# The last output tile in two halves added to a copied sum, and a newly fitted order of issue, in a fused attention and two-layer kernel

## The chip, the cores and the metric

The kernel runs on one NeuronCore of a Trainium2 chip. Times are microseconds (us) on the device. What counts is the median time of an execution. TensorE is called PE, its weight loads PEld, VectorE DVE, ScalarE ACT, GpSimd POOL and SyncE SP.

## The reference

Three steps follow each other. For batch 2, 8 heads, 768 positions and head size 64, block attention: each query sees the keys less than 16 positions away, and 24 summaries of blocks of 32 (the maximum of the keys, the mean of the values).

```
k_sum = k.reshape(B, H, nb, block, D).max(axis=3)
v_sum = v.reshape(B, H, nb, block, D).mean(axis=3)
mask_l = np.abs(pos[:, None] - pos[None, :]) < window
scores_all = np.concatenate([scores_l_m, scores_s], axis=-1)
a = np.exp(scores_all); a = a / (np.sum(a, axis=-1, keepdims=True) + 1e-09)
return np.matmul(a, v_all)
```

The result, as 1536 tokens of 512 features, goes through a gated layer of width 1536 and then through a second layer of width 2048:

```
xn = x / rms * rms_g
x = (silu(xn @ w_gate) * (xn @ w_val)) @ w_out
h = x @ w_in
out = where(h > 0, h, exp(min(h, 0)) - 1) @ w_out2
```

The weights are given in 64-bit floating point; activations and the output are in 32-bit.

## The kernel before

The 1536 tokens are three blocks of 512. `add_pair` does the attention of 128 queries (a pair of 64-query tiles, as two tiles of four heads): loads and transposes q, forms scores (`scores`, for the first four pairs on top of a mask laid in PSUM by `premask`), takes row maxima and exponentials, normalises (`normalize`), transposes (`turn_e`) and multiplies by v (`apply_v2`), and copies into the block's `xT`. The v windows are four buffers `va0` to `va3`, whose lower rows hold the block means; `place_v` puts the means into the first and `repeat_v` copies them on.

`add_norm` scales a block by the root of its mean squares. In the first block it works on two halves of 256 tokens: `square` (ACT) squares two groups of features at a time into two tiles, `sum_square` (PE) sums them over the features by products with ones, `root` (POOL) takes the power, `diagonal` (DVE) and `spread` (PE) lay it out over the features, and `scale_x` (DVE) multiplies. `SUMS = 2` says that for the halves PE sums both square tiles; with 1, `add_square` (POOL) adds the second tile to the first before.

`add_block1` and `add_block2` are the two layers. Every operand of a product is split into a rounded part and a rest (`split_a`, `split_b`, `x_hi`, `x_lo`, `act_a`, `act_b`), and each product is three (`THREE`): high by high, high by low, low by high. The first layer runs over 12 chunks of its width, the second over 16: a projection of 12 products of 512 columns, the nonlinear step, and `down`, 12 products that add onto the four accumulators `a0` to `a3` (one PSUM bank each). Weights arrive as 64-bit words and become 32-bit ones in three or four steps (`convert_a` on ACT, `convert_b` to `convert_d` on DVE). For the first two chunks of the first block the projections run by halves of 256 tokens, so that they can begin when the first half is scaled.

At the end of the third block the last two chunks (14 and 15) are put into the accumulators one accumulator after the other. `copy_out` copies each accumulator to an `ob` tile and `store` writes it. For the last one, `copy_out` is cut in two halves of 256 columns, one for ACT and one for DVE, with a store for each, both issued by SP.

The order of all work comes from a planner, `Order`, that runs on the host while the kernel is built. `add` hands it an operation with an engine (or a choice of engines with a duration each), a due time, what it reads and writes and the buffers that it takes. `issue` simulates the engines, takes on each free engine the ready operation that is due first, and writes the instructions in that order; on the chip each engine runs its own list in that order, and semaphores hold it back where data is missing. A load has a duration on the one modelled queue. The due times are moved by a table, `SHIFT`, with one entry for a kind of operation in one of ten stretches of due time (`EDGES`), and by constants such as `TOFF`, `T0`, `QL`, `WARM_AT`; `FLEX` says from which tile on `normalize` may be on ACT, too.

## Time and profile before

| | us |
|---|---|
| median of the runs shown (645.16, 645.78, 648.27) | 645.78 |
| profiled execution | 646.54 |
| span of the profiled execution | 644.8 |
| PE busy in the span | 630.3 (98%) |
| DVE, ACT, POOL busy | 454.8, 342.4, 95.6 |

The span goes from the first instruction to the last one; 1.74 us of the execution lie around it. A busy time is the sum of the instructions' own times; a PE that is busy is not always at its peak. In a row of a timeline, what stands in square brackets is the idle time before it and what ended it. The granted clock of TensorE in the table of stages is a share of 2.4 GHz.

### The profile page before, as it was taken

The page shows a single profiled execution, that of the slowest core. Times are in us where ns is not written, and L with a number is a line of the kernel's source. Part 1 is how long each engine was busy: PE and PEld are TensorE (multiplying, and loading weights), DVE is VectorE, ACT ScalarE, POOL GpSimd, SP SyncE. Part 2 cuts the span into 40 slices and gives each one's busy share as a digit, 9 for nine tenths or more (in the row PEclk, how much of TensorE's full clock was granted, in tenths as well). Part 3 has the DMA queues.
Part 4 walks back from the last instruction along what each step waited for, and adds up shares of the span by engine and source line. Part 5 has one row for each costly group of instructions (what it writes and reads, how often), then busy time and mean ns, then how long its engine had stood idle before and what let it go on. Part 6 is the DMA issues. An engine that isn't in the chain of part 4 may idle for free.

```text
span 644.8 us, 9843 instructions
## 1 busy us (share of the span) xinstructions
PE 630.3 (98%) x3644; PEld 516.3 (80%) x3644; DVE 454.8 (71%) x828; ACT 342.4 (53%) x739; POOL 95.6 (15%) x160
## 2 busy tenths in 40 slices
PE   7899999999999999999999999999999999999997
PEld 5678777788888888888888888888888888888885
DVE  4788878868964557499999975555765555855554
ACT  2797568975463633465555564434444444544442
POOL 5753356363210210000000000000000000000000
PEclk9999999999999999999999999999999999999999
DMA  9998858565500000025656300000010000100001
GB/s 217 243 225 211 213 156 237 179 137 176 162 1 0 2 1 0 2 67 180 185 166 207 110 1 1 1 1 1 1 65 1 1 1 1 65 1 1 2 0 66
DMA packets 80352, 52.94 MB, mean 82 GB/s; under 512 B 51504, under 2 KB 75312, under 8 KB 80304
## 3 DMA queue, kind: packets, MB, share of 16 engines
q1 hardware_dynamic: 80304, 52.31, 29.9%
q8 instruction: 29, 0.48, 0.3%
q14 instruction: 19, 0.16, 0.1%
HBM read 49.15 MB, written 3.15 MB: 81 GB/s over the span
## 4 chain that ended last, share of the span: by engine, by line
PE 84%; DVE 6%; DMA 3%; SPq 3%; ACT 2%; issue 1%; DVEq 0%; ACTq 0%
PE acc L967 34%; PE ph L899 20%; PE pg L899 13%; PE pv L728 1%; PE pv_7c L899 1%; PE pv_8c L899 1%; PE pv_9c L899 1%; PE pv_11c L899 1%; PE pv_10c L899 1%; PE s L676 1%; PE pv_4c L899 1%; DMA va<-in_v 1%; DMA st_o<-in_moe_w_out 1%; PE pv_6c L899 1%; PE pv_1c L899 1%
## 5 line engine op out<-in xcount | busy, mean ns | idle before, releaser
L899 PE MATMUL ph<-xb,ws_i 128*128 128x512 f32 x576 | 137.9, 389 | 0.0
L967 PE MATMUL acc<-ws_p,act 128*128 128x512 f32 x576 | 137.7, 389 | 0.0
L967 PEld LDWEIGHTS acc<-ws_p,act 128*128 128x128 f32 x576 | 108.1, 188 | 22.5
L899 PEld LDWEIGHTS ph<-xb,ws_i 128*128 128x128 f32 x576 | 108.1, 188 | 22.4
L899 PE MATMUL pg<-x,ws_g 128*128 128x512 f32 (+1 forms) x456 | 108.7, 383 | 1.6 <-DVE ws_g L313 0.9
L967 PE MATMUL acc<-act,ws_o 128*128 128x512 f32 x432 | 106.3, 392 | 0.0
L899 PEld LDWEIGHTS pg<-x,ws_g 128*128 128x128 f32 x456 | 81.5, 188 | 19.1 <-DVE ws_g L313 1.3
L967 PEld LDWEIGHTS acc<-act,ws_o 128*128 128x128 f32 x432 | 80.4, 188 | 17.1 <-issue 0.5
L939 ACT ACTIVATE ex<-ph 128x512 f32<-128x512 f32 x48 | 28.8, 599 | 105.0 <-PE ph L899 105.0
L943 DVE TENSOR_SCALAR ex<-ex 128x512 f32<-128x512 f32 x48 | 20.5, 427 | 87.5 <-ACT ex L939 87.5
L302 ACT CAST act<-ex 128x512 fp32r<-128x512 f32 x48 | 29.8, 620 | 21.6 <-DVE ex L947 21.6
L302 ACT CAST ws_v<-raw_v 128x512 fp32r<-128x512 f32 x36 | 22.3, 620 | 32.6 <-PE acc L967 9.7
L932 DVE SCALAR_TENSOR_TENSOR th<-th,pg 128x512 f32<-128x512 f32 x36 | 24.6, 684 | 20.5 <-ACT th L928 20.3
L313 DVE TENSOR_TENSOR ws_i<-raw_i,ws_i 128x512 fp32r<-128x512 f32 x48 | 33.1, 689 | 8.0 <-ACT ws_i L302 8.0
L302 ACT CAST ws_i<-raw_i 128x512 fp32r<-128x512 f32 x48 | 29.7, 620 | 12.1 <-PE acc L967 12.1
L928 ACT ACTIVATE th<-pg 128x512 f32<-128x512 f32 x36 | 21.4, 595 | 26.7 <-PE pg L899 26.6
L313 DVE TENSOR_TENSOR act<-ex,act 128x512 fp32r<-128x512 f32 x48 | 33.1, 689 | 3.2 <-ACT act L302 0.7
L947 DVE SCALAR_TENSOR_TENSOR ex<-ph,ex 128x512 f32<-128x512 f32 x48 | 33.2, 691 | 1.5
L313 DVE TENSOR_TENSOR ws_p<-raw_p,ws_p 128x512 fp32r<-128x512 f32 x48 | 32.8, 682 | 1.2 <-ACT ws_p L302 1.2
L302 ACT CAST ws_p<-raw_p 128x512 fp32r<-128x512 f32 x48 | 29.6, 616 | 6.7 <-PE acc L967 6.7
L313 DVE TENSOR_TENSOR ws_o<-raw_o,ws_o 128x512 fp32r<-128x512 f32 x36 | 27.7, 770 | 6.3 <-ACT ws_o L302 6.2
L302 ACT CAST ws_o<-raw_o 128x512 fp32r<-128x512 f32 x36 | 22.3, 620 | 16.1 <-PE acc L967 3.5
(214 smaller groups left out, 918.8 us busy)
## 6 DMA issues: line engine op xcount, KB each, us to landing
st_i<-in_moe_w_in SPq DMA_DIRECT2D x16, 512.0 KB, 3.9
st_p<-in_moe_w_out SPq DMA_DIRECT2D x16, 512.0 KB, 3.8
st_g<-in_moe_w_gate SPq DMA_DIRECT2D x12, 512.0 KB, 4.9
st_o<-in_moe_w_out SPq DMA_DIRECT2D x12, 512.0 KB, 5.5
st_v<-in_moe_w_val SPq DMA_DIRECT2D x12, 512.0 KB, 4.9
va<-in_v SPq DMA_DIRECT2D x20, 192.0 KB, 5.6
kr<-in_k SPq DMA_DIRECT2D x12, 256.0 KB, 5.0
out<-ob SPq DMA_DIRECT2D x11, 256.0 KB, 2.0
```

The lines of the kernel that those rows point to most:

```text
L302: nc.scalar.copy(out=out, in_=in_)
L313: (nc.gpsimd if eng == POOL else nc.vector).tensor_sub(out, a, b)
L676: nc.tensor.matmul(pq[h][ts, pr, :], qb[hs, pr, ts], ka[n][hs, pr, :], start=not pre, stop=not pre or pr == NP - 1)
L728: nc.tensor.matmul(pv[64 * h:64 * h + 64, pr, n, :], va[:NK, 2 * pr + h, :], T[f"ats{b}_{j}_{h}"][:, pr, QT * n:QT * n + QT], start=True, ...
L899: nc.tensor.matmul(pt[:, i], wt[:, a, kk * P:(kk + 1) * P], xt[:, c, kk, i], start=(kk == 0 and n == 0), stop=(kk == KM - 1 and n == 2))
L928: nc.scalar.activation(out=new("t2", f"th{b}_{c}", [P, TB]), in_=T[f"pg{b}_{c}"], func=AF.Tanh, scale=0.5)
L932: nc.vector.scalar_tensor_tensor(th, th, 1.0, T[f"pg{b}_{c}"], op0=ALU.add, op1=ALU.mult)
L939: nc.scalar.activation(out=new("t2", f"ex{b}_{c}", [P, TB]), in_=T[f"ph{b}_{c}"], func=AF.Exp)
L943: nc.vector.tensor_scalar(ex, ex, 1.0, -1.0, op0=ALU.min, op1=ALU.add)
L947: nc.vector.scalar_tensor_tensor(ex, T[f"ph{b}_{c}"], 0.0, ex, op0=ALU.max, op1=ALU.add)
L967: nc.tensor.matmul(acc, lhsT, rhs, start=(first and n == 0), stop=(last and n == 2))
```

## The change

For the last tile (rows 384 to 511 of the third block), the products of chunk 15 go into two banks of their own, 256 columns each (`down_part`). The accumulator, then complete for the other fifteen chunks, is copied to `ob` in one piece, and `add_part` adds each half to the copy. The first half is stored by SP and the second by ACT.

The planner's duration of a load is raised: weights 1.52 to 1.56 and 1.64 to 1.72, q and (for the second batch) k 1.18 to 1.25, a window of v 0.95 to 1.05; that of `convert_d` 0.6 to 0.63. All the constants and the table of shifts are new. `SUMS` is 1, `FLEX` 8 instead of 10 (so that `normalize` for one more pair is for POOL alone), and `LO_0` has the rests of w_val in the first block on POOL alone, where the twelve of the profile were before as well.

```diff
-        add("SP", 1.52 if kind in "op" else 1.64, need - (14 if need > T0 + 20 else LEAD), fetch, kind, c, w=[st], new=[("st", st)])
+        add("SP", 1.56 if kind in "op" else 1.72, need - (14 if need > T0 + 20 else LEAD), fetch, kind, c, w=[st], new=[("st", st)])
...
-        add("SP", 0.95, due, load_v, b, t, w=[va + "#a"])
+        add("SP", 1.05, due, load_v, b, t, w=[va + "#a"])
...
+    def down_part(x, act, ws):
+        ot, wt = T[act], T[ws]
+        pt, cs = new(MM, f"end{x}", [P, TB // 2]), slice(x * TB // 2, (x + 1) * TB // 2)
+        for n, (a, e) in enumerate(THREE):
+            nc.tensor.matmul(pt, ot[:, a, 3 * P:], wt[:, e, cs], start=n == 0, stop=n == 2)
+
+    def add_part(x, ob):
+        out = T[ob][:, x * TB // 2:(x + 1) * TB // 2]
+        nc.vector.tensor_add(out, T[f"end{x}"], out)
...
-    def store(src, r0, cs):
-        nc.sync.dma_start(out=out[r0:r0 + P, cs], in_=T[src][:, cs])
+    def store(src, r0, cs, by):
+        (nc.scalar if by == ACT else nc.sync).dma_start(out=out[r0:r0 + P, cs], in_=T[src][:, cs])
...
+            add_down(names, act, ws, False, c == C2 - 1, False, due, [(m,) for m in range(3)])
+            if c == C2 - 2:
+                add_down(names, act, ws, False, True, False, due + 4.08, [(3,)])
+            else:
+                for x in range(2):
+                    add(PE, 0.36, due + 6 + 0.3 * x, down_part, x, act, ws, r=[act + "#h", act + "#l", ws + "#h", ws + "#l"],
+                        w=[f"end{x}"], new=[(MM, f"end{x}")])
...
-                where = ANY if parts == 1 else ({ACT: 0.27}, {DVE: 0.33})[x]
-                add(where, 0, end + 0.3 * m, copy_out, names[m], ob, cs, r=[names[m], ob], w=[f"{ob}#{x}"])
-                add("SP", 0.73, end + 2, store, ob, b * TB + m * P, cs, r=[f"{ob}#{x}"])
+            add(ANY, 0, end + 0.3 * m, copy_out, names[m], ob, slice(0, DM), r=[names[m], ob], w=[f"{ob}#{x}" for x in range(parts)])
...
+            for x in range(2):
+                add(DVE, 0.35, end + 2 + 0.3 * x, add_part, x, ob, r=[f"end{x}"], w=[f"{ob}#{x}"])
+                by = ("SP", ACT)[x]
+                add(by, 0.4, end + 2 + 0.3 * x, store, ob, r0, slice(x * DM // 2, (x + 1) * DM // 2), by, r=[f"{ob}#{x}"])
...
-FLEX, NORM, KEYS = 10, 1, 0
+FLEX, NORM, KEYS = 8, 1, 0
...
-SUMS = 2
+SUMS = 1
```

What the new order does on an engine's list is shown at four places. The first is ACT's list after the exponentials of the first pair (`e_1_0` and `e_1_1` are the two tiles of the second pair, `va` the v windows, `ats` a transposed tile). Before:

```order
L693 ACTIVATE e_1_0_427,ss_1_0_468<-s_1_0_339,nm_1_0_453 128x120 x4
L302 COPY va_137<-va_136 24x512
L302 COPY va_139<-va_136 24x512
L693 ACTIVATE e_1_1_428,ss_1_1_513<-s_1_1_420,nm_1_1_462 128x120 x4
L693 ACTIVATE e_2_0_553,ss_2_0_596<-s_2_0_449,nm_2_0_581 128x120 x4
```

After:

```order
L693 ACTIVATE e_1_0_424,ss_1_0_464<-s_1_0_346,nm_1_0_449 128x120 x4
L693 ACTIVATE e_1_1_425,ss_1_1_490<-s_1_1_417,nm_1_1_458 128x120 x4
L302 COPY va_138<-va_136 24x512
L302 COPY ats_1_0_603<-at_1_0_581 120x512
L693 ACTIVATE e_2_0_559,ss_2_0_605<-s_2_0_443,nm_2_0_588 128x120 x4
```

The second exponentials of the pair have moved ahead of the copies into the windows, one copy has gone to POOL, and a copy of a transposed tile has come in. The second place is DVE's list from the diagonal of the first half (`dg`) to its last x_lo (`x`; `raw` are weights, `nm` row maxima). Before:

```order
L827 TENSOR_SCALAR dg0slice(0, 256, None)_767<-ident,y0slice(0, 256, None)_749 128x128 x2
...
L847 SCALAR_TENSOR_TENSOR xT_387<-xT_387,g_sb,prs0slice(0, 256, None)_780 128x256 x4
L884 TENSOR_TENSOR x_799<-xT_387,x_799 128x256
L435 TENSOR_SCALAR raw_g_825<-st_g_511 128x512
...
L682 SCALAR_TENSOR_TENSOR e_4_1_808<-s_4_1_806,mask_157 128x480
L686 TENSOR_REDUCE nm_4_0_866<-e_4_0_807 128x4
L686 TENSOR_REDUCE nm_4_1_889<-e_4_1_808 128x4
L682 SCALAR_TENSOR_TENSOR e_5_0_871<-s_5_0_869,mask_158 128x480
L682 SCALAR_TENSOR_TENSOR e_5_1_872<-s_5_1_870,mask_158 128x480
L884 TENSOR_TENSOR x_799<-xT_387,x_799 128x256 x3
```

After:

```order
L827 TENSOR_SCALAR dg0slice(0, 256, None)_809<-ident,y0slice(0, 256, None)_764 128x128 x2
L448 SCALAR_TENSOR_TENSOR raw_g_781<-st_g_516,raw_g_781 128x512
L448 SCALAR_TENSOR_TENSOR raw_v_771<-st_v_586,raw_v_771 128x512
L682 SCALAR_TENSOR_TENSOR e_4_0_791<-s_4_0_789,mask_157 128x480
L847 SCALAR_TENSOR_TENSOR xT_296<-xT_296,g_sb,prs0slice(0, 256, None)_814 128x256 x4
L682 SCALAR_TENSOR_TENSOR e_4_1_792<-s_4_1_790,mask_157 128x480
L686 TENSOR_REDUCE nm_4_0_868<-e_4_0_791 128x4
L686 TENSOR_REDUCE nm_4_1_888<-e_4_1_792 128x4
L884 TENSOR_TENSOR x_840<-xT_296,x_840 128x256 x4
```

Pair 5's two mask additions no longer stand in this stretch. The third place is POOL's list around the root of the second half (`y0slice(256, 512, None)`; L708 normalises). Before:

```order
L313 TENSOR_TENSOR ws_v_862<-raw_v_778,ws_v_862 128x512
L628 MEMSET va_139 32x512
L817 TENSOR_TENSOR y0slice(256, 512, None)_949<-ms0slice(256, 512, None)_943,mhalf 128x2
L313 TENSOR_TENSOR ws_g_1003<-raw_g_978,ws_g_1003 128x512
L708 TENSOR_TENSOR e_4_0_807<-e_4_0_807,rs_4_0_1055 128x480
```

After:

```order
L313 TENSOR_TENSOR ws_v_830<-raw_v_771,ws_v_830 128x512
L628 MEMSET va_139 32x512
L799 TENSOR_TENSOR  1)slice(256, 512, None)_909<- 1)slice(256, 512, None)_909, 3)slice(256, 512, None)_928 128x512
L708 TENSOR_TENSOR e_4_0_791<-e_4_0_791,rs_4_0_940 128x480
L708 TENSOR_TENSOR e_4_1_792<-e_4_1_792,rs_4_1_959 128x480
L817 TENSOR_TENSOR y0slice(256, 512, None)_980<-ms0slice(256, 512, None)_975,mhalf 128x2
```

The addition of squares has come in, and two normalisations have moved ahead of the root. In the same stretch PE's list has, behind the first projections, the transposes of the first two key tiles of the second batch and pair 4's transposes and products, which stood behind the second halves' projections before. The fourth place is the end of PE's list (`acc_2_3` is the last accumulator, `act_2_15` chunk 15). Before:

```order
L967 MATMUL acc_2_2_5632<-ws_p_6069,act_2_14_6119 128x512 x3
L967 MATMUL acc_2_2_5632<-ws_p_6108,act_2_15_6138 128x512 x3
L967 MATMUL acc_2_3_5636<-ws_p_6069,act_2_14_6119 128x512 x3
L967 MATMUL acc_2_3_5636<-ws_p_6108,act_2_15_6138 128x512 x3
L1245 UNCONDITIONAL_BRANCH
```

After:

```order
L967 MATMUL acc_2_2_5620<-ws_p_6096,act_2_15_6126 128x512 x3
L967 MATMUL acc_2_3_5624<-ws_p_6078,act_2_14_6107 128x512 x3
L974 MATMUL end_6158<-ws_p_6096,act_2_15_6126 128x256 x3
L974 MATMUL end_6164<-ws_p_6096,act_2_15_6126 128x256 x3
L1271 UNCONDITIONAL_BRANCH
```

Three products of 512 columns have become six of 256. On DVE's list four copies of 512 columns and then the two additions follow each other there.

## Rows read from the trace of the kernel before

**Rows 1.** Stages: stretch, length, busy us of each engine, clock, DMA share, GB/s
```profile
0.00:21.00 21.00, 16.44 (x185) 10.97 (x185) 9.87 (x26) 8.08 (x28) 13.69 (x58) 1.00 1.10 211
21.00:46.50 25.50, 23.24 (x389) 18.57 (x389) 21.54 (x54) 21.04 (x79) 15.57 (x27) 1.00 0.91 246
46.50:130.00 83.50, 79.96 (x650) 65.42 (x646) 68.95 (x138) 63.67 (x169) 35.99 (x49) 1.00 0.77 200
130.00:640.60 510.60, 510.60 (x2430) 421.38 (x2429) 354.00 (x610) 249.25 (x466) 30.40 (x29) 1.00 0.16 49
640.60:644.80 4.20, 0.05 (x1) 0.00 (x0) 0.42 (x1) 0.37 (x1) 0.00 (x0) 1.00 0.36 125
```
**Rows 2.** The chain that ended last, first 66 us: start, duration, what
```profile
14.54 6.40 DMA va<-in_v
...
22.70 1.14 ACT va L302 x2
...
32.69 1.68 PE 0slice(0, 256, None)_704 L806 x16
...
37.60 1.66 DVE xT L847 x4
...
44.74 1.00 DVE x L884 x3
```
**Rows 3.** Timeline of DVE, 22 to 62 us: start, duration, line, operation, tiles
```profile
25.36 0.57 DVE L699 TENSOR_SCALAR ss<-ss 128x4 f32<-128x4 f32 x1
...
28.96 0.16 DVE L699 TENSOR_SCALAR ss<-ss 128x4 f32<-128x4 f32 x1
...
43.52 1.22 DVE L682 SCALAR_TENSOR_TENSOR e<-s,mask 128x480 f32<-128x480 f32 x2
```
**Rows 4.** Timeline of PE, 23 to 75 us
```profile
30.37 1.05 PE L676 MATMUL s<-ka,qT 64*64 64x120 f32 x32
...
43.58 0.61 PE L806 MATMUL lice(256, 512, None)_903<-ones,lice(256, 512, None)_891 128*128 128x4 f32 x4 [0.17 <-ACT lice(256, 512, None)_891 L794]
...
45.53 1.08 PE L570 MATMUL vp<-vtok,sel 128*32 128x128 f32 x32
46.54 1.69 PE L899 MATMUL pg<-x,ws_g 128*128 128x256 f32 x12
...
51.62 2.89 PE L899 MATMUL pg<-x,ws_g 128*128 128x256 f32 x22 [0.52 <-POOL ws_g L313]
54.35 1.60 PE L899 MATMUL pv_0c<-x,ws_v 128*128 128x256 f32 x12
55.79 1.60 PE L899 MATMUL pg<-x,ws_g 128*128 128x256 f32 x12
```
**Rows 5.** Groups by line and shape: busy us and mean ns, idle before
```profile
L708 POOL TENSOR_TENSOR e<-e,rs 128x480 f32<-128x480 f32 x20 | 20.6, 1036 | 51.0 <-ACT th L928 30.4 <-DVE rs L703 18.9 <-ACT ws_g L302 1.0
...
L799 POOL TENSOR_TENSOR slice(0, 512, None)_2976<-slice(0, 512, None)_2976,slice(0, 512, None)_2986 128x512 f32<-128x512 f32 x1 | 1.3, 1292 | 0.1
```
**Rows 6.** Timeline of POOL, 22 to 62 us
```profile
46.30 0.71 POOL L817 TENSOR_TENSOR lice(256, 512, None)_949<-lice(256, 512, None)_943,mhalf 128x2 f32<-128x2 f32 x1 [1.27 <-DVE lice(256, 512, None)_943 L811]
```
**Rows 7.** What PE waited for, 0 to 150 us: total, times, longest
```profile
PE at L716 <- POOL ws_g L313: 1.0, 1, 1.0
...
PE pg L899 <- DVE ws_g L313: 0.9, 1, 0.9
```
**Rows 8.** The chain that ended last, from 625 us on
```profile
632.49 8.17 PE acc L967 x36
...
641.20 0.37 ACT ob L302
```
**Rows 9.** Timeline, 632 to 645 us
```profile
639.33 0.69 DVE L304 COPY ob<-acc 128x512 f32<-128x512 f32 x1 [0.67 <-PE acc L967]
640.69 0.42 DVE L304 COPY ob<-acc 128x256 f32<-128x256 f32 x1 [0.67 <-PE acc L967]
```
**Rows 10.** Timeline of SP's queue, 641 to 645 us
```profile
641.60 0.81 SPq L982 DMA_DIRECT2D out<-ob  x2
```

More of the change, by code (lines that the diff above doesn't have):

```diff
@@ new lines @@
+    ('load_turned', 0): -1, ('max_k', 0): 10.5, ('mean_own', 0): 6, ('mean_square', 0): 3.5,
+    ('normalize', 0): 6, ('place_v', 0): 14, ('project', 0): -7, ('project_f32', 0): -0.5,
+    ('repeat_v', 0): 13.5, ('root', 0): -11.5, ('scale_x', 0): -5.5, ('scores', 0): -26.5, ('split_a', 0): -3,
+    ('square', 0): -15, ('store', 0): -2.5, ('sum_square', 0): -1.5, ('take', 0): -8, ('turn_e', 0): 2.5,
+    ('turn_here', 0): 1, ('turn_k', 0): -4, ('turn_q', 0): 1.5, ('x_hi', 0): -6.5, ('x_lo', 0): 6,
@@ new lines @@
+    ('scores', 1): -3.5, ('split_a', 1): -3.5, ('split_b', 1): -16.5, ('spread', 1): 0.5, ('square', 1): 2,
+    ('store', 1): 7.5, ('take', 1): -7, ('turn_e', 1): 3.5, ('turn_here', 1): 3, ('turn_k', 1): 0.5,
+    ('turn_q', 1): -4, ('wait', 1): -12, ('x_hi', 1): 10, ('x_lo', 1): -6.5, ('zero_v', 1): 17,
+    ('act_a', 2): 1, ('act_b', 2): -7.5, ('add_mask', 2): -15, ('add_square', 2): 4, ('apply_v', 2): 7.5,
+    ('apply_v2', 2): 2.5, ('convert_a', 2): 6, ('convert_b', 2): -2.5, ('convert_c', 2): 1,
@@ new lines @@
+    ('split_b', 3): -33.5, ('spread', 3): 0.5, ('square', 3): -10, ('store', 3): -10, ('sum_square', 3): 4,
+    ('take', 3): -16, ('turn_e', 3): 15.5, ('turn_here', 3): 8, ('turn_k', 3): -4.5, ('turn_q', 3): -9.5,
+    ('wait', 3): 0.5, ('x_hi', 3): -1, ('x_lo', 3): -8, ('zero_v', 3): 1, ('act_a', 4): 3, ('act_b', 4): 8,
+    ('add_mask', 4): -1, ('add_square', 4): 1, ('apply_v', 4): -8, ('apply_v2', 4): -1,
+    ('convert_a', 4): -0.5, ('convert_b', 4): 7, ('convert_c', 4): 4.5, ('convert_d', 4): 1,
@@ new lines @@
+    ('project_f32', 6): 0.5, ('repeat_v', 6): 4, ('root', 6): -2.5, ('row_max', 6): -2, ('scale_x', 6): 8.5,
+    ('scores', 6): 5.5, ('split_a', 6): -4, ('split_b', 6): 1.5, ('spread', 6): -2, ('square', 6): 6,
+    ('store', 6): -8, ('sum_square', 6): -8, ('take', 6): 2, ('turn_e', 6): 8, ('turn_here', 6): 8,
+    ('turn_q', 6): -4.5, ('wait', 6): 1, ('x_hi', 6): -1.5, ('x_lo', 6): -1, ('zero_v', 6): 4,
+    ('act_a', 7): -6.5, ('act_b', 7): -16.5, ('add_mask', 7): -6, ('add_part', 7): -1, ('add_square', 7): 1,
@@ new lines @@
+    ('load_turned', 7): 2, ('load_v', 7): 6, ('load_vs', 7): -2, ('load_vtok', 7): -1.5, ('max_k', 7): -8,
+    ('mean_own', 7): -5.5, ('normalize', 7): -12, ('premask', 7): 14.5, ('project_f32', 7): 3,
+    ('repeat_v', 7): 2.5, ('root', 7): -3.5, ('row_max', 7): -4, ('scale_x', 7): 3, ('scores', 7): 2,
+    ('split_a', 7): -11.5, ('spread', 7): -6, ('store', 7): 5, ('take', 7): -4.5, ('turn_e', 7): 2,
+    ('turn_q', 7): -1, ('x_hi', 7): -1.5, ('zero_v', 7): 7, ('act_a', 8): 5, ('act_b', 8): 15.5,
```

240 lines of the change are left out of this document (111 added, 129 removed).

## The prediction

> **What bounds the kernel now.** I read the table of stages first: five stretches with the busy time of each engine [rows 1]. The reader is to see where TensorE (PE) is idle. From 130 to 640.6 us it is busy for all 510.60 us. Up to 130 us it is busy for 16.44 + 23.24 + 79.96 us, so it idles 4.56 us before 21 us, 2.26 us up to 46.5 us and 3.54 us up to 130 us. After its last product 4.2 us pass. So the time is PE's work, plus 10.4 us of early idling, plus the tail. An edit counts if it takes PE work away, if it shortens the early idling, or if it shortens the tail; vector and scalar work in the long middle is worth nothing.
>
> Then the chain that ended last, in order of time. Up to 21 us it is loads: the fourth window of v lands at 20.94 us after 6.40 us under way [rows 2], and PE's sums over it wait for that. From there to about 46 us it runs through ScalarE (ACT) and VectorE (DVE) work on the first query pairs and the norm. At 46.54 us the first projection starts [rows 4], and PE mostly sets the pace. The end of the chain is PE, DVE, ACT and a store [rows 8 to 10].
>
> **The change part by part.** Durations are those of the profiled execution, 646.54 us with a span of 644.8; the median of the runs shown is 645.78, 0.76 us less. I subtract from both alike.
>
> *Start to 21 us.* The same fourteen loads stand ahead of the same landing (six of k, two of q, two halves of v, four windows); only their order inside is changed. The three pairs of warming products in front of the first transposes stand in time in which PE waits for k. I cost both at nothing; the cover is the landing at 20.94 us [rows 2].
>
> *Sums of squares.* In the first block each half now adds its two squares on GpSimd (POOL) first, so PE does half the products. The first half's take 1.68 us in the chain [rows 2]; the second half's begin at 43.58 us and give way to the next products at 45.53 us, 1.9 us, and end before the projection at 46.54 [rows 4]. Half of each is 0.84 + 0.95 = 1.8 us less PE work. Against it stand two POOL additions of 1.29 us, as one of the same shape took [rows 5]. The first stands in the chain of the first half: 1.29 added, 0.84 saved. I hold that this is covered: on ACT the exponentials of the second pair no longer stand behind two copies into the v windows (1.14 us [rows 2]), so everything behind them starts about that much earlier. 1.14 + 0.84 - 1.29 leaves 0.7 us to the good, which I don't count, since DVE's order decides next.
>
> *DVE ahead of the first projection.* Before, from the scaling of the first half (37.60 us) to the end of its last x_lo (44.74 + 1.00 = 45.74 us) DVE needs 8.14 us [rows 2]. In that stretch the additions of the mask for pair 5 took 1.22 us [rows 3]. These now stand far behind the projections, and one integer step of a weight has gone ahead of the diagonal. The rest is the same. So the last x_lo comes at least 1.2 us earlier, about 1.5 with the step: near 44.2 us.
>
> *What PE has to do until then.* Ahead of the first projection PE loses 0.84 (first half's sums), the scores of pair 5 (1.05 us, as an earlier pair's took [rows 4]) and the second half's 1.9 us, and gains about 0.3 of v sums: 3.5 us less, so it would be done at 46.54 - 3.5 = 43.0 us. It therefore waits for DVE until about 44.2. The scores and 0.95 us of sums are still owed then. 44.2 + 2.0 = 46.2 against 46.54: a gain of 0.3 us if DVE is as I say; if DVE is not in the way, 43.0 + 2.0 = 45.0: 1.5 us. I take 1.0, nearer to neither end, because ACT's earlier exponentials also bring the norm's start forward and that I did not count. Bounds: 0 and 1.5.
>
> *The second half of the norm.* Its root now stands on POOL behind the addition (1.29 us) and two normalisations (1.04 us each, the mean of twenty [rows 5]), where before it ran at 46.30 us as soon as it was ready [rows 6]. That is up to 3.4 us later. Behind it wait DVE's diagonal and scaling, and PE's second-half projections, which begin at 51.62 us before [rows 4]. PE has been handed cover: two transposes of k, pair 4's transposes and products and a projection of 12 products (1.60 us, as the row of its kind [rows 4]) stand there now, some 4.5 us. I cost it at nothing; without the cover it would be 3.4 us.
>
> What POOL's additions do to DVE is told by a row first: the same small DVE step took 0.57 us while POOL normalised and 0.16 us when POOL was not in the way [rows 3]. The Trainium skill, "SBUF — State Buffer", section "Who interferes with whom", says that the port pair which VectorE and GpSimd share is an exclusive lock for a whole instruction. By that rule both additions of squares would block DVE in full, and the sum would lose up to twice 1.29 us; it is a rival below.
>
> *46.5 to 130 us.* The tables that give each operation its due time are new throughout, and the planner now holds a weight load, a q or k load and a v window for 0.04 to 0.1 us longer on the queue. So the order of products and of weight preparation differs at most places of the first two blocks. PE's waits there before are few: 0.9 us for a weight's low part from DVE, 1.0 for one from POOL, 0.5 at 51.62 us [rows 4, 7]. No row tells which of these stay. I take the change as 0.3 us less, with bounds of the whole 3.5 us of idling either way [rows 1].
>
> *The tail.* Before, the last accumulator is ready when PE ends, 632.49 + 8.17 = 640.66 us [rows 8]. DVE copies one half for 0.42 us from 640.69 [rows 9], ACT the other from 641.20 for 0.37 [rows 8], and only then does the SP queue issue both stores, from 641.60 on, 0.81 us together [rows 10]: the second starts near 642.0. After: the sum of the other fifteen chunks is complete at 640.66 - 0.68 = 639.98. DVE is still copying the third accumulator (639.33 + 0.69 = 640.02 [rows 9]), then copies this one in 0.69 to 640.73, then adds the halves. An addition of this shape from PSUM is not in the trace; the nearest rows are the copy of 128x256 from PSUM, 0.42 [rows 9], and the subtraction of 128x256 in SBUF, 1.00 / 3 = 0.33 [rows 2]. I take 0.42 as it too reads PSUM. The halves are ready at 641.17 and 641.61, and the second is issued by ACT at about 641.65 with nothing ahead of it. 642.0 - 641.65 = 0.35 us. PE itself does six products of 256 columns, 1.44 / 12 = 0.12 us apart (54.35 to 55.79), for three of 512 at 0.227 (8.17 / 36): 0.04 more, hidden under DVE's copy. A store issued by ACT is not in the trace; if its issue takes as long as both on SP (0.81 instead of 0.4 [rows 10]), 0.1 is lost, and 0.45 is the best; I take 0.3, since ACT has nothing else to do there. The Trainium skill, "DMA: Bandwidth & Descriptors", section "Issuing engines are not separate DMA queues", says that issuing on several engines saves only the sequencer's time to issue. By that only the 0.4 us between the two issues is to be had, whatever DVE does; the sum would still be 0.3.
>
> **Sum:** 1.0 + 0.3 + 0.3 = 1.6 us. 646.54 - 1.6 = 644.9 for the profiled execution, 645.78 - 1.6 = 644.2 for the median.
>
> **The rivals.**
> - *The early idling goes too.* If the new order also ends half of the 2.26 + 3.54 us of idling [rows 1], 2.9 us more: 644.2 - 2.9 = 641.3. For it: all of it is waits for other engines' order, none is for a bound. Against: no single one is longer than 1.0 us [rows 7].
> - *Slower: the second half's norm comes late.* POOL's queue delays the root by 3.4 us and the cover of 4.5 us is used up by the lead that PE has won and by weights that are not ready. Then PE waits at the second-half projections: 645.78 - 0.3 (tail) - 1.0 + 3.4 = 647.9. It decides once the second half's scaled input comes more than about 1 us after PE reaches it, near 52 us.
> - *The lock.* Both POOL additions block DVE for 1.29 us each in the stretch where DVE sets the pace: 644.2 + 2.6 = 646.8. For it: the 0.57 against 0.16 us [rows 3]. Against: most of what DVE does there reads PSUM or one operand.
> - *The tail gives nothing.* DVE has three operations in a row, and two new waits; if the additions take as long as the issues they replace, 644.5.
>
> **How the numbers follow.** Forecast 0.47, idling gone 0.20, slower norm 0.13, lock 0.10, tail nothing 0.10. The range runs from 641.4, where most of the first rival is in, to 647.2, where the lock is in and the worst of the slower norm is out. About 0.5% (3.2 us) is what a measurement here can tell from no change. Faster than 642.55 is most of the first rival and a tail of the forecast: 0.22. Slower than 649.0 needs the norm rival and a late weight besides: 0.07. Within: 0.71.
>
> **What would show it.** Right: the first projection starts near 44 to 45 us and PE idles less than 1.5 us between there and 55 us; the sums of squares show half their rows; ACT issues one store and the last instruction of SP and ACT's stores lie within 0.5 us; the middle stays at full PE. Wrong: PE waits over 1 us for x at the second-half projections, or DVE operations beside POOL's addition run to 1.3 us, or PE's idle time before 130 us differs from 10.4 us by more than 3.

## The result, and the profile after

The kernel after takes 653.3 us in the median (five runs, 652.61 to 654.38). The kernel before took 645.86 us beside it. The ratio of the means is 1.0100, with a 95% interval of 1.0069 to 1.0132: the change costs 6.5 us (4.5 to 8.5). The profiled execution took 654.38 us with a span of 651.3, which is 6.5 us more than the span before. The forecast was 1.6 us faster, and its range ended at 647.2.

The stages of after (columns as in [rows 1]):

```profile
0.00:21.00 21.00, 17.54 (x173) 11.15 (x177) 9.32 (x26) 7.07 (x22) 12.65 (x56) 1.00 1.13 213
21.00:46.50 25.50, 21.73 (x372) 16.54 (x365) 20.70 (x52) 20.28 (x77) 18.28 (x30) 1.00 0.97 254
46.50:130.00 83.50, 77.35 (x615) 63.17 (x614) 67.85 (x128) 58.45 (x150) 41.67 (x51) 0.98 0.72 186
130.00:640.60 510.60, 509.07 (x2451) 419.38 (x2450) 357.84 (x620) 254.07 (x482) 28.02 (x32) 1.00 0.16 50
```

Beside [rows 1], PE idles 3.46 us up to 21 us (4.56 before), 3.77 up to 46.5 (2.26), 6.15 up to 130 (3.54) and 1.53 from there on (none before). Of the 3.0 us that came in before 130 us, most lie in the third stage. That stage also shows a granted clock of 0.98, where before had 1.00 everywhere. Over the whole span PE is busy for 632.65 us instead of 630.29. So the 6.5 us of the span are 4.5 us more of idling and 2.4 more of busy time, less 0.4 at the end. The single waits of PE up to 300 us tell where (what it waited for: total, times, longest):

```profile
PE kt L494 <- DMA kr<-in_k: 3.2, 3, 2.5
...
PE slice(0, 512, None)_2093 L841 <- DVE dg1slice(0, 512, None)l L835: 1.1, 1, 1.1
```

Of the 3.2 us, 2.49 are one wait at 77 us; the rest is at the start. Before, the longest behind 21 us was 1.0 us [rows 7]. Three places follow.

**A load that comes late.** `kt` is the transpose of a key tile `kr` of the second batch. PE's timeline (start, duration, what; idle time before it in brackets):

```profile
75.79 1.52 PE L899 MATMUL pv_2c<-x,ws_v 128*128 128x512 f32 x6
79.80 0.63 PE L494 MATMUL kt<-ident,kr 128*128 128x128 f32 x4 [2.49 <-DMA kr<-in_k]
80.19 2.60 PE L899 MATMUL pv_2c<-x,ws_v 128*128 128x512 f32 x6
```

After the wait, six products take 2.60 us instead of 1.52, and the clock says why (columns as in [rows 1]):

```profile
81.00:82.00 1.00, 1.00 (x4) 0.81 (x3) 0.00 (x0) 0.05 (x1) 0.51 (x1) 0.50 1.34 227
...
84.00:85.00 1.00, 1.00 (x6) 0.81 (x5) 0.81 (x3) 0.79 (x2) 0.00 (x0) 1.00 1.03 397
```

PE ran at 1.2 GHz from some 80.5 to 84 us, half of 2.4, so some 1.7 us went there (half of 3.5, an estimate). Why the keys are late stands on SP's list, which issues the loads. First SP of before, then of after:

```profile
43.32 6.37 SPq L486 DMA_DIRECT2D kr<-in_k  x3
49.79 1.42 SPq L415 DMA_DIRECT2D st_v<-in_moe_w_val  x1
...
76.14 2.70 SPq L486 DMA_DIRECT2D kr<-in_k  x3
```

```profile
43.21 1.83 SPq L486 DMA_DIRECT2D kr<-in_k  x1
47.57 0.39 SPq L415 DMA_DIRECT2D st_v<-in_moe_w_val  x1
53.68 0.35 SPq L412 DMA_DIRECT2D st_o<-in_moe_w_out  x1
...
71.99 4.22 SPq L502 DMA_DIRECT2D qr<-in_q  x8
76.25 3.07 SPq L486 DMA_DIRECT2D kr<-in_k  x4
```

The second batch has six key tiles. Before, SP issued the first three in one go, waited for nothing longer than 1.1 us from 43 to 53 us, and issued the other three at 76.14. After, two come early (37.40 and 43.21 us), then SP stands from 47.96 to 53.68, and the third tile comes with the last three only at 76.25, behind all that was queued after the stand. `st` has four buffers for raw weights, and a fetch has to wait until `convert_d` has read one of them for the last time. DVE's timeline of that stretch in after, and POOL's under it:

```profile
48.93 0.85 DVE L699 TENSOR_SCALAR ss<-ss 128x4 f32<-128x4 f32 x1 [1.13 <-ACT e L693]
...
50.39 1.48 DVE L313 TENSOR_TENSOR ws_o<-raw_o,ws_o 128x512 fp32r<-128x512 f32 x1
...
52.48 0.48 DVE L827 TENSOR_SCALAR lice(256, 512, None)_998<-ident,lice(256, 512, None)_980 128x128 f32<-128x128 f32 x2 [0.28 <-POOL lice(256, 512, None)_980 L817]
52.88 0.73 DVE L448 SCALAR_TENSOR_TENSOR raw_g<-st_g,raw_g 128x512 uint16<-128x512 uint16 x1
```

```profile
47.52 1.30 POOL L799 TENSOR_TENSOR lice(256, 512, None)_909<-lice(256, 512, None)_909,lice(256, 512, None)_928 128x512 f32<-128x512 f32 x1 [2.54 <-ACT lice(256, 512, None)_928 L794]
...
50.15 1.17 POOL L708 TENSOR_TENSOR e<-e,rs 128x480 f32<-128x480 f32 x1 [0.38 <-DVE lice(256, 512, None)_975 L811]
51.28 1.17 POOL L817 TENSOR_TENSOR lice(256, 512, None)_980<-lice(256, 512, None)_975,mhalf 128x2 f32<-128x2 f32 x1
```

The `convert_d` of w_gate's chunk 1 (L448, `raw_g`) ends at 53.61, and SP goes on at 53.68. It stands on DVE's list behind a wait of 1.13 us for ACT's exponentials, a split (L313) that takes 1.48 us beside a normalisation on POOL (0.67 without, in e_steps), and the second half's diagonal (L827). For the root (L817) DVE waits only 0.28 us. The root comes at 51.28 us, 5.0 later than before [rows 6]. Most of that is ACT's: it makes the half's squares at 46.25 us instead of 42.90, and POOL stands 2.54 us for them. Of the two normalisations (L708) ahead of the root only the second holds it up, for 1.0 us. PE itself waited only 0.83 us for that diagonal.

**A lock.** The wait of 1.1 us is at the norm of the second block. DVE lays out the high and low diagonals in four steps each; POOL's timeline stands under DVE's:

```profile
136.75 0.87 DVE L835 TENSOR_SCALAR dg1slice(0, 512, None)h<-ident,slice(0, 512, None)_2035 128x128 fp32r<-128x128 f32 x4
137.54 2.92 DVE L835 TENSOR_SCALAR dg1slice(0, 512, None)l<-ident,slice(0, 512, None)_2035 128x128 fp32r<-128x128 f32 x4
```

```profile
137.38 1.37 POOL L313 TENSOR_TENSOR ws_g<-raw_g,ws_g 128x512 fp32r<-128x512 f32 x1 [1.21 <-ACT ws_g L302]
138.72 1.26 POOL L313 TENSOR_TENSOR ws_v<-raw_v,ws_v 128x512 fp32r<-128x512 f32 x1
```

The same four steps take 0.87 us alone and 2.92 beside two subtractions on POOL. In before no split on POOL lies over the diagonals (they start at 140.8 us; the nearest splits at 135.0 and 145.1), and both rows read 0.87.

**The norm of the second half.** Between 48.8 and 56 us PE loses 2.2 us in four short waits (0.34, 0.33, 0.83, 0.72). The row of products that ends with the second half's first projection begins at 56.00 instead of 51.62 [rows 4], and ends at 59.24 instead of 54.51, though the first projection starts earlier than before (the row's other products are the first half's of the next chunk):

```profile
45.62 1.69 PE L899 MATMUL pg<-x,ws_g 128*128 128x256 f32 x12
...
56.00 3.24 PE L899 MATMUL pg<-x,ws_g 128*128 128x256 f32 x24
```

The end did what it should (timeline of after from 646 us):

```profile
646.68 0.87 PE L974 MATMUL end<-ws_p,act 128*128 128x256 f32 x6
647.68 0.76 DVE L978 TENSOR_TENSOR ob<-end,ob 128x256 f32<-128x256 f32 x2
648.47 0.38 ACTq L993 DMA_DIRECT2D out<-ob  x1
```

From PE's last product (646.68 + 0.87 = 647.55) to the end of the span are 3.75 us; before, 644.8 - 640.66 = 4.14 [rows 8].

### The profile page after: what moved, and what is told of

Its sections match the earlier page's. It is cut to its first block, busy times and chain, and to the rows that moved or that the text cites. A ratio compares the mean times of both kernels' runs of the same rounds, so it can differ in the third digit from the quotient of the medians.

```text
span 651.3 us, 9846 instructions
## 1 busy us (share of the span) xinstructions
PE 632.7 (97%) x3631; PEld 515.9 (79%) x3631; DVE 460.5 (71%) x828; ACT 340.5 (52%) x730; POOL 100.6 (15%) x166
## 4 chain that ended last, share of the span: by engine, by line
PE 82%; DVE 6%; DMA 6%; ACT 3%; SPq 1%; issue 1%; POOL 1%; DVEq 0%; ACTq 0%; POOLq 0%
PE acc L967 33%; PE ph L899 20%; PE pg L899 12%; DMA st_g<-in_moe_w_gate 2%; ACT e L693 2%; PE pv_6c L899 1%; PE pv_5c L899 1%; DMA kr<-in_k 1%; PE pv_8c L899 1%; PE pv_11c L899 1%; PE pv_10c L899 1%; PE pv_9c L899 1%; PE s L676 1%; DMA va<-in_v 1%; PE at L716 1%
## 5 line engine op out<-in xcount | busy, mean ns | idle before, releaser
L899 PE MATMUL ph<-xb,ws_i 128*128 128x512 f32 x576 | 139.3, 389 | 0.0
L313 DVE TENSOR_TENSOR ws_i<-raw_i,ws_i 128x512 fp32r<-128x512 f32 x48 | 32.9, 685 | 18.3 <-ACT ws_i L302 18.3
L313 DVE TENSOR_TENSOR ws_p<-raw_p,ws_p 128x512 fp32r<-128x512 f32 x48 | 33.1, 689 | 10.4 <-ACT ws_p L302 10.4
L313 DVE TENSOR_TENSOR act<-ex,act 128x512 fp32r<-128x512 f32 x48 | 33.1, 689 | 4.5 <-ACT act L302 0.7
L313 DVE TENSOR_TENSOR ws_o<-raw_o,ws_o 128x512 fp32r<-128x512 f32 x36 | 27.0, 750 | 8.4 <-ACT ws_o L302 8.3
```

The costliest lines, as they stand in the source:

```text
L313: (nc.gpsimd if eng == POOL else nc.vector).tensor_sub(out, a, b)
L899: nc.tensor.matmul(pt[:, i], wt[:, a, kk * P:(kk + 1) * P], xt[:, c, kk, i], start=(kk == 0 and n == 0), stop=(kk == KM - 1 and n == 2))
```

## The experiments

Most kernels are the kernel after with single operations moved. Where the planner has done its work, a short function moves an entry of the list of operations ahead of another (all engines keep the rest of their order), or gives an operation to another engine:

```diff
-        for i in started:
+        for i in arrange(ops, started, taken):
...
+    for src, dst in MOVES:
+        i = started.pop(at(src))
+        started.insert(at(dst), i)
+    for src, engine in GIVEN:
+        taken[started[at(src)]] = engine
```

The diffs below show the entries of `MOVES` (what, ahead of what) and `GIVEN`. Times are medians. Ratios are to the kernel before, which ran beside each group: 646.76, 646.85, 646.18 and 646.03 us. The kernel before scatters by some 4 us from run to run (644.58 to 649.32 in 23 runs), so ratios are compared.

### First group: which wait costs

**e_kt** leaves the late keys late and puts products ahead of their transposes, so that PE need not wait there.

```diff
+    (('project', 'pv0_2c', "('m0', 'm1')", 'ws0_v2', 'x0', '(2, 3)'), ('turn_k', '1', '2')),
+    (('project', 'pg0_3', "('m0', 'm1')", 'ws0_g3', 'x0', '(0, 1)'), ('turn_k', '1', '2')),
+    (('act_a', 'th0_2'), ('copy_k', '1', '3')),
...
```

> The new kernel; only the order around one wait is changed. PE stood 2.49 us at 77.3 us for the third key tile of the second batch (kr), whose load SP had issued at 76.25 us; here the second half of pv_2c and the first half of pg_3 stand ahead of that transpose (the act step of chunk 2 and its weight's low part are moved ahead of the copy and the maximum of the fourth key tile to match). Theory A (the wait and the fall of the granted clock to 0.50 that follows it at 81 us are this one place): PE's wait for kr falls under 0.5 us, the clock stays at 1.00 from 78 to 86 us, and the time is 653.3 - 2.5 - 1.8 = 649.0. Rival B (the wait moves on: PE, which comes earlier to the next chunk, waits there for weights, and nothing is won): 652.5 to 653.5. Rival C (the clock falls for another reason): wait gone, clock still 0.5 at 81 us, 650.8.

651.98 us, ratio 1.0093 [1.0067, 1.0120]; ten runs, five of 650.3 to 651.4 and five of 652.6 to 656.0. In its trace the wait is gone (PE, then a stretch of the clock):

```profile
81.12 1.03 PE L494 MATMUL kt<-ident,kr 128*128 128x128 f32 x8
```

```profile
55.00:60.00 5.00, 4.31 (x22) 4.26 (x21) 4.00 (x11) 3.25 (x7) 0.75 (x1) 0.50 0.97 249
```

But now the clock is at half from some 51 to 60 us, where nothing was moved and PE only had its short waits. That is not what makes some runs longer: the five shorter ones, the profiled one among them, have a mean granted clock of 0.991 or 0.992, the five longer ones 0.995 to 1.000. The kernel can't be told from after; what the wait at 77 us is worth is not settled by it.

**e_fill** keeps the wait and fills it with ten products that nobody reads, to keep the clock up.

```diff
+        for _ in range(10 if (b, i) == (1, 2) else 0):
+            nc.tensor.matmul(pt, idle_w, idle_w.unsqueeze(1).to_broadcast([P, 4, P]), start=True, stop=True)
```

> The new kernel with ten products that nobody reads put on PE ahead of that transpose of the third key tile, so that PE works where it stood 2.49 us; order and wait for the load are unchanged. Theory A (PE's standing makes the clock fall behind it): the transpose starts when it did, the granted clock stays at 1.00 from 80 to 85 us, and the time is 653.3 - 1.8 = 651.5. Rival C (the clock falls for another reason): 0.50 still, 653.3. If the ten products take longer than the wait, each 0.2 us too long is lost.

653.8 us, ratio 1.0095 [1.0061, 1.0130]: no gain that can be told. The clock did stay up behind the filled wait, and fell later in the same execution:

```profile
80.00:85.00 5.00, 5.00 (x27) 4.15 (x26) 4.55 (x8) 3.05 (x6) 0.49 (x1) 1.00 1.10 333
107.00:111.00 4.00, 4.00 (x11) 3.14 (x12) 4.00 (x11) 3.57 (x12) 1.92 (x4) 0.57 0.09 29
```

It is inconclusive on the clock's price.

**e_norm** moves the second half's norm forward on POOL, DVE and PE, with the steps of weights put behind it.

```diff
+    (('normalize', '0', '4_1'), ('turn_k', '1', '0')),
+    (('convert_d', 'g', '1'), ('convert_b', 'o', '1')),
+    (('diagonal', '0', 'slice(256, 512, None)'), ('convert_d', 'g', '1')),
+    (('spread', '0', 'slice(256, 512, None)'), ('turn_e', '0', '4_1')),
...
+    (('convert_d', 'v', '1'), ('convert_d', 'o', '1')),
...
```

> The new kernel; only the order around the second half's norm is changed: its root stands on POOL ahead of the second normalisation of pair 4, on DVE the diagonal, the scaling and x_lo stand ahead of a weight split and two weight steps, and on PE the spread stands ahead of that pair's second transposes. Theory A (this order costs PE what it idles from 50 to 56 us, 2.6 us): the second-half projections start near 54.3 instead of 56.0 us, time 651.6. Rival B (PE comes earlier and waits later, at the load of kr at 77 us, by as much more): 653.0 to 653.5, with the wait for kr at 4 us. By B the gain shows only together with e_kt.

657.63 us, ratio 1.0156 [1.0119, 1.0192]: 3.6 us slower than after by the ratios, where a gain was expected. The diagonal did come earlier (49.68 us, which is 5.5 behind the start of the first projection, where after has 6.9). But the `convert_d` of w_val's chunk 1, now behind the scaling, ran last at 59.70 on DVE, and SP stood for its buffer:

```profile
59.70 0.75 DVE L448 SCALAR_TENSOR_TENSOR raw_v<-st_v,raw_v 128x512 uint16<-128x512 uint16 x1
```

```profile
60.54 0.37 SPq L415 DMA_DIRECT2D st_g<-in_moe_w_gate  x1
```

PE waited 2.4 us for q in consequence, and still 2.1 for the keys (the rest of its waits for k is at the start, before 25 us). Its clock was at 0.75 from 46.5 to 60 us, where after has 1.00. This miss showed first that a step of weight preparation on DVE sets SP's loads.

**e_lock** takes the two splits that stand beside the diagonals from POOL and gives them to DVE, behind the diagonals.

```diff
+    (('split_b', '0', 'g', '8'), ('gate_b', '0', '7')),
+    (('split_b', '0', 'v', '8'), ('gate_b', '0', '7')),
+GIVEN = ((('split_b', '0', 'g', '8'), 'DVE'), (('split_b', '0', 'v', '8'), 'DVE'), )
```

> The new kernel; the two weight splits of chunk 8 that ran on POOL at 137.4 and 138.7 us, while DVE's four steps of the low diagonal (dg1 l) took 2.92 us instead of the 0.87 us of the four before, are given to DVE behind the diagonal. Theory A (POOL's two splits held DVE): the four steps take 0.87 us, PE's wait of 1.09 us for them at 140.5 us is gone, time 653.3 - 1.1 = 652.2. Rival D (the steps were slow for another reason, or DVE's two more splits of 0.68 us put the same wait on the nonlinear step behind): 653.0 to 653.6.

652.61 us, ratio 1.0077 [1.0052, 1.0102]; after had 1.0100, so some 1.5 us, within the scatter here. The trace of DVE is plain:

```profile
137.72 0.87 DVE L835 TENSOR_SCALAR dg1slice(0, 512, None)l<-ident,slice(0, 512, None)_2035 128x128 fp32r<-128x128 f32 x4
```

### Second group: SP's list, and the end alone

**e_kload** changes SP's list alone: the four key tiles are issued before the fetch that stands.

```diff
+    (('load_k', '1', '2'), ('fetch', 'o', '2')),
+    (('load_k', '1', '3'), ('fetch', 'o', '2')),
+    (('load_k', '1', '4'), ('fetch', 'o', '2')),
+    (('load_k', '1', '5'), ('fetch', 'o', '2')),
```

> The new kernel; on SP's list alone the four loads of k that PE waits for are moved ahead of the load of st_o, which SP issues at 53.68 us after standing since 47.96 us for a weight buffer that DVE frees at 53.6. Theory E (SP's standing is the root: the loads of k need no weight buffer, and standing behind it they push all later loads back by their 3.07 us): the loads fill the gap, PE's wait of 2.49 us for kr at 77 us and the half clock behind it go, the next weight of v is issued 3 us earlier, and no wait of the same size takes the place: 653.3 - 2.5 - 1.7 - 0.5 = 648.6. Rival B (it only moves on, to a wait behind the sixteen small loads of qr_2 near 98 us, where the runs with PE ahead of time lost 5 us between 95 and 110): 652 to 653.5.

649.14 us, ratio 1.0043 [1.0025, 1.0062]. As expected: 3.7 us of the 6.5 by ratios are gone (1.3 to 6.1, an estimate from the two intervals). The loads now fill SP's stand, the long wait is gone, and the clock is full from 77 to 90 us:

```profile
46.95 4.90 SPq L486 DMA_DIRECT2D kr<-in_k  x4
52.62 0.41 SPq L412 DMA_DIRECT2D st_o<-in_moe_w_out  x1
```

```profile
77.00:90.00 13.00, 12.44 (x65) 10.02 (x65) 10.67 (x19) 9.40 (x23) 6.71 (x10) 1.00 0.56 164
```

In after, the same stretch has PE busy for 10.51 us at a clock of 0.87.

**e_steps** comes from the other side: two `convert_d` go ahead of a split on DVE, so that SP's buffer is free earlier.

```diff
+    (('convert_d', 'g', '1'), ('split_b', '0', 'o', '0')),
+    (('convert_d', 'v', '1'), ('split_b', '0', 'o', '0')),
```

> The new kernel; on DVE's list alone the last steps of the weights g1 and v1 (0.73 and 0.75 us) stand ahead of a split, a weight step and the diagonal of the second half's norm instead of behind them, so that the buffers that SP waits for come free near 51.1 instead of 53.6 us. Theory E: SP issues st_o at 51.2, every load to 90 us comes some 2.4 us earlier, PE's wait for kr at 77 us falls to under 0.5: 653.3 - 2.0 - 1.7 + 0.4 (the diagonal comes that much later) = 650.0. Rival F (SP is bound by the rate of the loads from 54 us on and not by the gap): PE's wait for kr over 2 us, 653 to 654.

651.36 us, ratio 1.0078 [1.0046, 1.0111], less than expected. SP stood 3.83 us, from 46.51 to 50.34, instead of 5.72, which shows what it had stood for, and PE's wait of 2.49 us for the late key is gone:

```profile
50.34 0.35 SPq L412 DMA_DIRECT2D st_o<-in_moe_w_out  x1
```

But now the diagonal was late, and PE waited for it:

```profile
51.72 1.49 DVE L827 TENSOR_SCALAR ice(256, 512, None)_1000<-ident,lice(256, 512, None)_980 128x128 f32<-128x128 f32 x2
```

```profile
53.36 0.67 PE L841 MATMUL ice(256, 512, None)_1005<-ice(256, 512, None)_1000,ones 128*128 128x256 f32 x2 [2.71 <-DVE ice(256, 512, None)_1000 L827]
```

The diagonal took 1.49 us (0.48 in after), beside a split that POOL had begun at 51.87: the lock at a second place.

**e_all** is e_kload, e_steps and e_lock in one.

> The new kernel with the four loads of k ahead of st_o on SP, the two weight steps ahead of the split on DVE, and chunk 8's two splits on DVE behind the diagonal (as in three other runs, each by itself). Theory E: the gains add up but for what PE, coming earlier, meets next: 648.6 - 0.5 - 1.1 = 647.0, near the kernel before. Rival B: 651 or more.

649.79 us, ratio 1.0043 [1.0021, 1.0066]: what the splits' move gains, the late diagonal takes (again a wait of 2.7 us in its trace).

**e_tail** is the kernel before with after's code of the end, and before's table and durations.

> The kernel before with the change at the end alone: chunk 15's last products by halves into two banks, a copy of the other chunks' sum, two additions, one store from ACT; all tables and durations are those of before, so the order up to 625 us is the same. Theory A (the end is worth what the two profiles show, 4.14 us from the last accumulator to the end of the span before and 3.75 after): 0.4 us faster than before, ratio 0.9994. Rival (the end gives nothing or costs): ratio 1.000 or above. A difference of 0.4 us is below what the times tell apart here, so the profile's end decides: the last product to the end of the span.

645.91 us, ratio 0.9982 [0.9964, 0.9999], 1.2 us (0.1 to 2.3) faster than before, and the only kernel here that beats both. Its PE ends at 640.96 + 0.87 = 641.83, 3.77 us before the end of its span of 645.6:

```profile
640.96 0.87 PE L974 MATMUL end<-ws_p,act 128*128 128x256 f32 x6
```

By the trace the end gains 4.14 - 3.77 = 0.37 us; the interval holds that.

### Third group: parts together, and the sums in the old order

**e_klock** is e_kload and e_lock.

> The new kernel with two of the changes tried singly: the four loads of k ahead of st_o on SP, and chunk 8's two weight splits on DVE behind the diagonal; the two weight steps stay where they are. Theory: the diagonal's low part takes 0.87 instead of 2.93 us, PE's wait of 1.1 us for it goes, and 649.1 - 1.3 = 647.8 (in the run with all three, 1.5 us instead of 2.7 were lost from 130 to 150 us, against 0.2 in the kernel before). Rival: that run was no faster than the one with the loads alone, because the gain at 140 us is eaten later, where vector work binds: 649.1.

647.63 us, ratio 1.0021 [1.0008, 1.0034], as expected. Against e_kload this is 0.0022, 1.4 us for the lock, which by the two intervals may be nothing up to 2.9; against after, 5.1 of 6.5 us (2.9 to 7.3) are undone by moving six operations. The wait of 1.1 us is gone from its trace as from e_lock's.

**e_fix** adds to e_klock the moves of e_norm, and a split on ACT put earlier.

```diff
+    (('split_a', '0', 'g', '1'), ('copy_e', '0', '4_1')),
```

> The last, and the second half's norm put in front: its root on POOL ahead of pair 4's second normalisation, on DVE the diagonal, scaling and x_lo ahead of a split and two weight steps, on ACT the high part of g1 ahead of a copy, on PE the spread ahead of that pair's second transposes and one key transpose behind a projection. The loads of k fill SP's time, so a later free buffer costs it little (without them this order cost 4 us, by SP's standing). Theory: the second-half projections start 1.4 us earlier than in the last one, near 53.5, PE loses about 2 instead of 3.5 us from 46.5 to 55, and the time is 647.8 - 1.4 = 646.4, that of the kernel before. Rival (what comes earlier there waits again for weights or loads before 110 us): 647.8 or above.

650.97 us, ratio 1.0069 [1.0052, 1.0087]: 3 us slower than e_klock, a miss. With the keys out of the way, the stand still held q:

```profile
52.13 0.98 SPq L412 DMA_DIRECT2D st_o<-in_moe_w_out  x1
59.52 0.37 SPq L415 DMA_DIRECT2D st_g<-in_moe_w_gate  x1
```

```profile
64.38 1.12 PE L482 MATMUL qt<-ident,qr 128*128 128x128 f32 x4 [3.12 <-DMA qr<-in_q]
```

**e_sums** is the kernel before with the squares of the first block added on POOL and summed by PE once, as in after, in before's order.

```diff
+        if blk == 0 and cs == SQ[0][1]:
+            add_square(blk, cs, i)
...
-            parts = [(cs, n) for cs in SQ[blk][:n_sums] for n in range(TB // w)]
+            parts = [(cs, n) for cs in SQ[blk][:1] for n in range(TB // w)]
```

> The kernel before with one thing changed: in the first block POOL adds the second tile of squares to the first for each half, right behind ACT's square, and PE sums one tile instead of two (the planner's order is that of before, with the two additions put in). The prediction's term by itself: PE has 1.8 us less work, each addition stands in the chain for 1.29 us less the 0.84 to 0.95 saved. Theory A (PE's own work counts there): 0.5 to 1.0 us faster than before, ratio near 0.9988. Rival G (the addition comes later than the sums it saves, and its chain sets the start of the first projection): the first projection starts 0.4 us later, ratio 1.000 to 1.002.

653.07 us, ratio 1.0098 [1.0072, 1.0123]: 6.3 us slower, where a small gain was expected. PE waits for each addition, and is at half clock for a while after both (PE, then the clock):

```profile
34.48 1.26 PE L808 MATMUL 0slice(0, 256, None)_705<-ones,)slice(0, 256, None)_674 128*128 128x4 f32 x8 [1.32 <-POOL )slice(0, 256, None)_674 L801]
...
49.86 1.87 PE L808 MATMUL lice(256, 512, None)_901<-ones,lice(256, 512, None)_888 128*128 128x4 f32 x8 [2.32 <-POOL lice(256, 512, None)_888 L801]
```

```profile
35.00:42.00 7.00, 7.00 (x54) 6.04 (x54) 2.68 (x11) 3.59 (x12) 2.82 (x4) 0.51 0.90 231
48.00:56.00 8.00, 6.14 (x53) 5.64 (x54) 6.80 (x15) 7.08 (x29) 3.47 (x5) 0.57 1.11 215
```

The second addition stands behind two splits on POOL (46.08 and 47.31 us). The clock has a large share of the price in this execution: 7.00 x 0.49 + 6.14 x 0.43 = 6.1 us of PE's time in these two rows would not be there at full clock (an estimate from the rows).

**e_tailsums** is e_sums and e_tail in one.

> The kernel before with the change at the end and the addition of squares, both of the parts of the change that can be told apart from the tables. Theory A: 1.2 us for the end, as measured by itself, and 0.5 to 1.0 for the squares: ratio near 0.997. Rival G: the end alone, ratio 0.998 or above.

649.25 us, ratio 1.0047 [1.0027, 1.0068]; against e_tail the sums cost 0.0065, 4.2 us. It shows the same two waits (1.3 and 2.3 us), and a clock of 0.80 and 0.79 where e_sums has 0.51 and 0.57.

### Fourth group: the norm without the stand, and the sums in the new order

**e_fix2** is e_fix with the `convert_d` that held SP put ahead of the scaling, and one copy on ACT moved.

```diff
-    (('convert_d', 'v', '1'), ('convert_d', 'o', '1')),
+    (('convert_d', 'v', '1'), ('scale_x', '0', '0', 'slice(256, 512, None)')),
+    (('copy_x2', '0', '4'), ('copy_k', '1', '1')),
```

> The kernel with the loads of k ahead and chunk 8's splits on DVE (647.6 us by itself), and the second half's norm put in front as in the run before, but with both weight steps that free SP's buffers still ahead of the scaling, and with the block's x_hi ahead of the copy of pair 4's product on ACT. Theory A (the norm's order costs what PE loses there, less what the dependencies leave): the second-half projections start 0.8 to 1.2 us earlier than at 54.9, SP does not stand for more than 1 us, PE does not wait for qr, time 646.5 to 646.9. Rival B (the time is taken back before 110 us): 647.6 or above.

647.46 us, ratio 1.0020 [1.0008, 1.0031]. Against e_fix, 0.0049 or 3.2 us come back, and SP's stand is gone, with the wait for q down to 0.59 us:

```profile
52.43 0.37 SPq L415 DMA_DIRECT2D st_g<-in_moe_w_gate  x1
```

But it is no faster than e_klock (1.0021). The moves hardly bring the second half forward: its first projection begins at 55.79 us, and the next one (`pv_0c`) at 57.30, where e_klock has 57.60.

```profile
55.79 1.68 PE L899 MATMUL pg<-x,ws_g 128*128 128x256 f32 x12
```

So what an earlier norm would be worth is not tested by this run.

**e_sq2** is e_klock without the addition on POOL in the first block; PE sums both square tiles, as in before.

```diff
-        nc.gpsimd.tensor_add(s, s, T[f"sq{blk}_{cs}{i}"])
+        blk and nc.gpsimd.tensor_add(s, s, T[f"sq{blk}_{cs}{i}"])
...
-            parts = [(cs, n) for cs in SQ[blk][:n_sums] for n in range(TB // w)]
+            parts = [(cs, n) for cs in SQ[blk][:n_sums if blk else 2] for n in range(TB // w)]
```

> The kernel with the loads of k ahead and chunk 8's splits on DVE (647.6 us by itself), with the addition of squares of the first block undone: PE sums both tiles of squares for each half (sixteen small products instead of eight), POOL adds nothing there; all else in the order of the new kernel. Theory H (the addition on POOL costs more than PE's saved work, as in the order of before): 646 to 647. Rival A, the prediction's own term (PE has 1.8 us more work, of which about 1.0 counts): 648.6.

647.14 us, ratio 1.0018 [0.9996, 1.0040]. In the new order the addition is worth nothing that can be told, either way.

## Why the prediction was wrong

- **46.5 to 130 us: the step that failed.** It was sized at 0.3 us less, "with bounds of the whole 3.5 us of idling either way". That bound has a lower end by its nature (idling can't fall below nothing) and none above: idle time of before says nothing of waits that a new order brings. PE idles 2.6 us more there, and runs at half clock for some 3.5 us behind the longest wait. The step read PE's waits and never SP's list, although the part on the change says that the planner holds loads longer on that queue. The order of SP alone would have shown it: before, three of the second batch's key tiles are issued ahead of the next fetches of weights; after, two are, and the third stands with the others behind fetches that wait for buffers and behind sixteen small loads of q. e_kload, which changes nothing but the place of these loads, gives 3.7 of the 6.5 us back.
- **The second half's norm: a delay from another list, and another reader.** The root was forecast "up to 3.4 us" later, for POOL's queue alone, and costed at nothing because PE had cover for 4.5 us. It came at 51.28 instead of 46.30 [rows 6], 5.0 us later. Of these, 3.35 are ACT's squares (46.25 instead of 42.90), a list that the step did not read; 0.6 are the addition less the shorter sums, and 1.0 POOL's second normalisation. That the delay was near the forecast is in good part luck. PE's cover mostly held: its wait for the diagonal was 0.83 us. The step also took the row at 51.62 us for the second half's projections; ten of its products are still the next chunk's first half, for whose weight PE waits there, and the second half's twelve come behind them. What was not asked is what else is queued on DVE in that stretch. It was the last step of a weight, and behind that a buffer, and behind that SP with the keys. e_norm, e_steps and e_fix against e_fix2 each moved such a step, and SP's next issue moved with it. The rival "slower: the second half's norm comes late" named the place, but most of the price came by another way. What the late norm costs PE by itself is not shown: e_fix2 brings the second half forward by only 0.3 us against e_klock, and gains nothing.
- **The lock: the right rule at the wrong place.** The rival put it at the two additions of squares, where e_sq2 finds no price that can be told. It struck the diagonals of the second block, 2.92 us instead of 0.87, and e_klock against e_kload gives some 1.4 us for it, e_lock against after 1.5. The Trainium skill, "SBUF — State Buffer", section "Who interferes with whom", names `tensor_scalar` among the DVE instructions that can take the shared port pair, and says that whoever issues first keeps it for the whole instruction. The trace agrees: two of POOL's subtractions (1.37 and 1.26 us) lie over the steps, and these are 2.05 us longer. So "against: most of what DVE does there reads PSUM or one operand" was no shield: the steps that were held read one tile. And the prediction looked for the lock only around new instructions, not around old ones that the order had put beside each other, and held that vector work past 130 us is worth nothing; PE idles 1.53 us there in after.
- **Sums of squares.** That PE saves half is right (eight rows of products in the second half, 1.05 us). That the time falls by it is not shown: e_sq2 finds no difference. "Covered" hung on the new order: in before's order the same edit cost 6.3 us (e_sums) and 4.2 (e_tailsums).
- **DVE ahead of the first projection.** Forecast near 44 to 45 us; 45.62 in after, 43.98 to 44.82 in the profiles of e_lock, e_steps, e_kload, e_all, e_klock and e_fix2, whose start is the same. This step held, with 0.9 us in after and up to 2.6 in the others (single executions differ: e_tail, with the start of before, has 48.16 against 46.54); but the lead was lost again by 56 us. The term of 1.0 us was taken where PE starts, not where it next waits.
- **Start to 21 us**: forecast as unchanged. PE's idle time there fell by 1.1 us in after, but in the profiles with the same start it lies between 2.98 (e_kload) and 5.08 us (e_all), so that no change can be told.
- **The tail**: 0.3 us forecast, 4.14 - 3.75 = 0.39 in after and 0.37 in e_tail. An addition took 0.76 / 2 = 0.38 us (0.42 forecast), ACT's issue 0.38 us (0.4).

By ratios the 6.5 us are 3.7 for the keys behind SP's stand, shown by a run that undoes this alone, and some 1.4 for the lock, where two pairs of runs agree and the traces show the wait gone, but neither time alone tells it from nothing. 1.4 us (0.5 to 2.2) remain between e_klock and before. Since the end alone gains 0.4 (trace) to 1.2 us (times), the new order owes 1.8 to 2.6 us that no run undoes. In e_klock's trace PE is busy for 11.16 us from 46.5 to 60, as in after (11.14), where before has 12.84: 1.7 us more of idling, of the size of what remains, but not shown to be it. What would bring it back stays open.

## What to carry to other kernels

When an order is changed, read the list of the engine that issues the loads as closely as that of the engine that sets the pace: an issue that waits for a buffer holds every later load, also those that need no buffer. For each wait that a change makes longer, follow what is queued behind the waiting instruction until a list ends in a load. And a bound from the idle time of before holds for gains only; what a new order can lose has to be bounded by its own lists.
